# Fetching the second feed-forward block's weights at most 8 units ahead instead of 60

## The chip, the cores and the metric

The kernel runs on one core of one Trainium2 chip. Its time is the device time of one execution, in microseconds (us). Before the change three runs took 660.59, 662.50 and 663.89 us; the median is 662.5 us. Five parts of the core appear below: PE (TensorE, matrix multiplication), DVE (VectorE), ACT (ScalarE), POOL (GpSimd) and SP (SyncE, which here only issues DMA transfers).

## The reference

Attention with a position bias is followed by two feed-forward blocks over 1152 tokens of width 512, all in float32:

```python
attn = softmax(q k^T / 8 + bias(log-distance MLP)) @ v      # 2 batches, 8 heads, 576 positions, 64 wide
x    = attn, laid out as 1152 x 512
h    = x @ w_in                                              # 512 -> 2048
x    = (h * clip(h + 3, 0, 6) / 6) @ w_out                   # 2048 -> 512
xn   = x / sqrt(mean(x*x) + 1e-6) * rms_g
out  = (silu(xn @ w_gate) * (xn @ w_val)) @ w_out2           # 512 -> 1536 -> 512
```

The weights arrive as float64 arrays, and the kernel reads them as pairs of 32-bit integers.

## The kernel before

Tokens are cut into three blocks of 384 (n = 0, 1, 2), and the inner width of each feed-forward block into slices of 128 (16 slices in the first block, 12 in the second). A unit is one token block with one slice. There are 84 units: 0 to 47 belong to the first block, 48 to 83 to the second. Each block first goes through its slices with n = 0 and 1 (units 48 to 71 in the second block, two units to a slice) and then with n = 2 (units 72 to 83).

Every product is computed with operands split into a high and a low part (`wh`, `wl` for weights; `nh`, `nl` for the normalised tokens; `gh`, `gl` for the inner activations), as high x high, high x low and low x high. In the second block a unit therefore works as follows.

- Line 701 (`first`): 12 matmuls of 384 columns for the gate slice into a PSUM tile `h`, then 12 more for the value slice into another. Only two `h` tiles exist and they are used in turn.
- Line 729: ACT computes silu of the gate tile into `r`, which frees that `h` tile. Line 733: DVE multiplies `r` with the value tile, which frees the second one.
- Line 710: ACT makes `gh` out of `r`; line 713: DVE makes `gl`.
- Line 746 (`second`): 9 matmuls of 512 columns with the output weights. They are issued one unit late, so PE's order is gate and value of unit i, then the output matmuls of unit i-1, then gate and value of unit i+1.

Weights have to be converted from float64 to `wh` and `wl` before use. One weight tile of 128 x 512 is one transfer of 512 KB (line 110) into one of three `raw` buffers, and then goes through a small pipeline of turns, one stage a turn: ACT takes the absolute value of the upper words (line 130); DVE does three integer operations on it (lines 138, 139 and 143), the last of which frees the raw buffer; ACT rounds it to `wh` (line 122) and POOL subtracts to get `wl` (line 151). A turn carries at most one weight tile in each stage. A unit of the second block has two turns. In the first, lines 138, 139 and 143 stand on DVE ahead of line 733. In the second, lines 138 and 139 stand between lines 733 and 713, and line 143 behind line 713. If no weight is pending, the turn leaves these operations out.

Which weight is pending is decided while the program is built. 29 slots hold converted weights. After each unit, `weight_want` (lines 183 to 203) looks at the units from now on, up to `far` of them, for the first weight that is in no slot, picks the slot whose content is needed last, and issues the transfer. It goes on until three weights are pending. A slot whose content is needed again is taken only where the new weight is needed within 8 units (`near`).

In units 49 to 57 there is further work for the tokens of block n = 2, which reach the second block later than the others: three copies on DVE (line 768) beside ACT squares after unit 49, a square root on ACT, which needs a table load and another back to silu at line 729 (after unit 50), five tiny operations and three scalings on DVE (lines 784 to 796, after unit 51), and after each of the units 54 to 57 three transposes on PE (line 804, shown as `xnT`), then `nh` on ACT (line 805) and `nl` on DVE (line 810). These transposes take an `h` tile. So there the gate matmuls of the next unit wait for line 733 of this one, and its value matmuls wait for line 810.

All of this is written out in a fixed order for each engine.

Of the kernel before, what the change touches and what calls it, by code (L numbers as in the profile page):

```python
# [48 lines left out]
def kernel(ctx, tc, q, k, v, w1, b1, w2, w_in, w_out, w_gate, w_val, w_out2, rms_g, dtab, ntab, itab, out):  # L49
# [43 lines left out]
    pend = []  # L93
# [11 lines left out]
    def weight_load(wid, s):  # L105
        raw = wst.tile([128, 512, 2], I32, tag="raw", name="raw")
        dst = raw.rearrange("p c z -> p (c z)")
        if wid[0] in "igv":
            dst = dst.rearrange("p (k f) -> p k f", k=4)
        nc.sync.dma_start(out=dst, in_=weight_src(wid))  # L110
        pend.append((wid, s, raw, turn_no[0]))
# [68 lines left out]
    def next_use(w, u):  # L180
        return next((x for x in uses[w] if x >= u), INF)

    def weight_want(now, near, far):

        for u in range(now, min(now + far, len(seq))):
            for w in seq[u]:
                if w in where:
                    continue
                best, dist = None, -1
                for s, h in enumerate(holds):  # L190
                    d = INF + 1 if h is None else next_use(h, now)
                    if d > dist and (d >= INF or (d > u and u - now <= near)):
                        best, dist = s, d
                if best is None:
                    return False
                if holds[best] is not None:
                    del where[holds[best]]
                    slot_of.pop(holds[best], None)
                holds[best] = w
                where[w] = best  # L200
                weight_load(w, best)
                return True
        return False

    def weight_need(u):
        for w in seq[u]:
            assert w in where, (u, w)
            while not (w in slot_of and slot_of[w][2] == where[w]):
                late_turns.append((u, w))
                conv_turn()  # L210
# [11 lines left out]
    if True:  # L222
# [575 lines left out]
        def norm_5(n, c):  # L798
            if n < 2:
                ps = ps_y.tile([128, BT], F32, tag="yb", name="xnT")  # L800
            else:
                ps = ps_h.tile([128, BT], F32, tag="h", name="xnT")
            for t in range(3):
                transpose(ps[:, t * 128:(t + 1) * 128], xn_t[n, t][:, c * 128:(c + 1) * 128])
            nc.scalar.activation(out=x_t[1, n][0][:, c, :], in_=ps, func=ACTF.Copy, scale=rg[:, c:c + 1])
            return ps

        def norm_6(n, c, ps):
            h_, l_ = x_t[1, n]
            nc.vector.scalar_tensor_tensor(  # L810
                out=l_[:, c, :], in0=ps, scalar=rg[:, c:c + 1], in1=h_[:, c, :], op0=ALU.mult, op1=ALU.subtract,
            )
# [21 lines left out]
        def finish(ph, n, f, g):  # L834
            F = (F1, F2)[ph]
            last = (ph, n, f) == units[-1]
            second("ou"[ph], ph, n, f, F, g, last)
            if f == F - 1 and not last:
                if ph == 0:
                    late1.append(None)  # L840
                    late1.extend(part(norm_1, n, t) for t in range(3))
                    late1.append(None)
                    late.extend([None, None, part(norm_2, n)])
                    late.append(None)
                    late.append(part(norm_3, n))
                    late.extend(part(norm_4, n, t) for t in range(3))
                    late.append(None)
                    late.append(None)
                    late.append(lambda: turn.extend((n, c) for c in range(4)))
                else:  # L850
                    late1.append(None)
                    late1.extend(part(final, n, t) for t in range(3))

        def late_step():

            for q in (late1, late):
                while q and q[0] is not None:
                    q.pop(0)()
                if q:
                    q.pop(0)  # L860

        queue = []
        with tc.manual_schedule():
            for i, (ph, n, f) in enumerate(units):
                weight_need(i)
                g = (unit1, unit2)[ph](n, f)
                queue.append((ph, n, f, g))
                while len(queue) > (2 if ph == 0 else 1):
                    finish(*queue.pop(0))
                if turn:  # L870
                    x = turn.pop(0)
                    norm_6(*x, norm_5(*x))
                late_step()
                while len(pend) < 3 and weight_want(i + 1 - len(queue), 8, 60):
                    pass
            for x in queue:
                finish(*x)
            while late or late1:
                late_step()
# [31 lines left out]
```

## Time and profile before

| | |
|---|---|
| median of three runs | 662.5 us |
| the profiled execution's own time | 662.26 us |
| its span in the profile | 660.5 us |
| PE busy | 633.3 us (96%) |
| DVE busy | 479.8 us (73%) |
| ACT busy | 342.6 us (52%) |
| POOL busy | 144.7 us (22%) |
| unit 48, first matmul | 417.56 us |
| weight tiles converted | 86 |

The span is the time from the first to the last instruction that the profile holds; all times in the rows below count from its start. Matmuls overlap each other in the pipeline, so PE's busy time says less than the distance between the starts of its matmuls. The TensorE clock was granted in full in the whole span (0.999).

### The profile page before, as it was taken

To read this page: it belongs to the slowest core of one execution; us is meant where nothing else is said; L and a number is where in the kernel's file an instruction comes from. 1 tells how busy PE (TensorE), PEld (TensorE's weight loads), DVE (VectorE), ACT (ScalarE), POOL (GpSimd) and SP (SyncE) were. 2 spreads that over 40 slices of the span, in tenths; PEclk is the share of its full clock that TensorE was granted. 3 is DMA by queue.
4 is the path that set the end of the run, shared out by engine and by line. 5 is a ranking of instruction groups with operands and counts; after the bars stand their busy time and mean duration, and the time that the engine had idled before them with its cause. 6 is when DMAs were issued, how large, how long until landed. Compare 5 with 4: busy or idle time off the path is not lost.

```text
span 660.5 us, 11012 instructions
## 1 busy us (share of the span) xinstructions
PE 633.3 (96%) x4174; PEld 525.0 (79%) x4174; DVE 479.8 (73%) x885; ACT 342.6 (52%) x675; POOL 144.7 (22%) x117
## 2 busy tenths in 40 slices
PE   5699999999999999999999999999899999999997
PEld 2256656656777999999999989998789999999996
DVE  6687799758656799888843799989993552498512
ACT  5867766677556555555534555574542331354311
POOL 1000010013110243333310023333441130044300
PEclk9999999999999999999999999999999999999999
DMA  6999958537500144333320124444452230146101
GB/s 153 282 287 239 266 164 261 131 80 204 140 3 1 55 139 133 127 126 126 128 64 1 33 96 128 143 149 129 153 160 65 79 114 1 63 153 230 34 0 49
DMA packets 75250, 80.69 MB, mean 122 GB/s; under 512 B 23996, under 2 KB 59964, under 8 KB 75196
## 3 DMA queue, kind: packets, MB, share of 16 engines
q1 hardware_dynamic: 75196, 79.98, 40.8%
q8 instruction: 33, 0.54, 0.3%
q14 instruction: 21, 0.17, 0.1%
HBM read 66.71 MB, written 13.25 MB: 121 GB/s over the span
## 4 chain that ended last, share of the span: by engine, by line
PE 80%; DVE 11%; DMA 3%; issue 3%; ACT 1%; SPq 1%; DVEq 0%; ACTq 0%
PE h L701 33%; PE ya L746 16%; PE yb L746 8%; PE pv L490 6%; PE tps L86 6%; PE s L427 6%; PE bps L357 4%; DVE wm L139 2%; DVE e L441 1%; DVE wm L143 1%; DVE wm L138 1%; DMA bias<-biasd 1%; PE qps L86 1%; DMA raw<-in_moe_w_out_dram 1%; DVE R L344 1%
## 5 line engine op out<-in xcount | busy, mean ns | idle before, releaser
L151 POOL TENSOR_TENSOR wl<-wm,wh 128x512 fp32r<-128x512 f32 x86 | 126.4, 1470 | 301.1 <-ACT wh L122 176.2
L143 DVE SCALAR_TENSOR_TENSOR wm<-raw,wm 128x512 int32<-128x512 int32 x86 | 127.5, 1482 | 0.9
L710 ACT CAST gh<-r 128x384 fp32r<-128x384 f32 x84 | 43.2, 514 | 118.0 <-DVE r L733 71.2
L701 PE MATMUL h<-nh,wh 128*128 128x384 f32 x288 | 97.6, 339 | 5.1 <-DVE r L733 3.2
L701 PE MATMUL h<-nh,wl 128*128 128x384 f32 x288 | 96.7, 336 | 0.0
L701 PE MATMUL h<-nl,wh 128*128 128x384 f32 x288 | 96.5, 335 | 0.0
L441 DVE CUSTOM_DVE_ANT_1 e<-s,bias 128x576 f32<-128x576 f32 x72 | 54.3, 755 | 29.8 <-PE tps L86 17.7
L733 DVE TENSOR_TENSOR r<-r,h 128x384 f32<-128x384 f32 x36 | 19.9, 551 | 66.6 <-PE h L701 66.3
L452 ACT ACTIVATE e<-e,m 128x576 f32<-128x576 f32 x72 | 56.0, 778 | 19.8 <-DVE m L441 19.8
L701 PE MATMUL h<-xh,wh 128*128 128x384 f32 x192 | 65.4, 341 | 0.0
L701 PE MATMUL h<-xh,wl 128*128 128x384 f32 x192 | 64.7, 337 | 0.0
L139 DVE SCALAR_TENSOR_TENSOR wm<-raw,wm 128x512 int32<-128x512 int32 x86 | 62.5, 727 | 2.9
L701 PE MATMUL h<-xl,wh 128*128 128x384 f32 x192 | 64.4, 336 | 0.0
L701 PEld LDWEIGHTS h<-nh,wh 128*128 128x128 f32 x288 | 54.1, 188 | 8.6 <-DVE r L733 4.0
L130 ACT ACTIVATE wm<-raw 128x512 f32<-128x512 f32 x86 | 58.0, 674 | 5.1 <-DMA raw<-in_moe_w_in_dram 2.2
L713 DVE TENSOR_TENSOR gl<-r,gh 128x384 fp32r<-128x384 f32 x84 | 46.6, 554 | 15.6 <-ACT gh L710 15.6
L427 PE MATMUL s<-kS,q 64*128 64x288 f32 (+1 forms) x320 | 54.6, 449 | 2.7 <-DVE m L441 2.7
L86 PEld LDWEIGHTS tps<-ident,e 128*128 128x128 f32 x324 | 42.5, 200 | 18.2 <-issue 8.9
L86 PE MATMUL tps<-ident,e 128*128 128x128 f32 x324 | 55.9, 297 | 0.1
L344 DVE TENSOR_SCALAR R<-T,NB 128x368 f32<-128x368 f32 (+17 forms) x124 | 54.0, 485 | 2.2 <-PE bps L357 1.7
L122 ACT CAST wh<-wm 128x512 fp32r<-128x512 f32 x86 | 52.9, 617 | 4.7 <-DVE wm L143 4.7
L701 PEld LDWEIGHTS h<-nl,wh 128*128 128x128 f32 x288 | 54.1, 188 | 1.4
(102 smaller groups left out, 1079.6 us busy)
## 6 DMA issues: line engine op xcount, KB each, us to landing
raw<-in_moe_w_out_dram SPq DMA_DIRECT2D x33, 512.0 KB, 3.6
biasd<-ev SPq DMA_DIRECT2D x36, 295.5 KB, 4.1
raw<-in_moe_w_gate_dram SPq DMA_DIRECT2D x19, 512.0 KB, 3.5
raw<-in_moe_w_in_dram SPq DMA_DIRECT2D x18, 512.0 KB, 3.6
bias<-biasd SPq DMA_DIRECT2D x15, 576.0 KB, 5.4
raw<-in_moe_w_val_dram SPq DMA_DIRECT2D x16, 512.0 KB, 3.6
rawq<-in_q_dram SPq DMA_DIRECT2D x32, 128.0 KB, 3.3
bias<-biasd SPq DMA_DIRECT2D x10, 288.0 KB, 4.9
```

The source lines that it names most:

```text
L86: nc.tensor.transpose(out, in_, ident[:n, :n])
L122: nc.scalar.copy(out=hi, in_=m)
L130: nc.scalar.activation(out=m, in_=raw[:, :, 1].bitcast(F32), func=ACTF.Abs, scale=2.0 ** -112)
L139: nc.vector.scalar_tensor_tensor(out=m, in0=raw[:, :, 0], scalar=29, in1=m, op0=ALU.logical_shift_right, op1=ALU.bitwise_or,)
L143: nc.vector.scalar_tensor_tensor(out=m, in0=raw[:, :, 1], scalar=-0x80000000, in1=m, op0=ALU.bitwise_and, op1=ALU.bitwise_or,)
L151: nc.gpsimd.tensor_tensor(out=lo, in0=m, in1=hi, op=ALU.subtract)
L344: nc.vector.tensor_scalar(out=R, in0=src, scalar1=NB1[:, col], scalar2=None, op0=ALU.max)
L427: nc.tensor.matmul(s[sl, r, :SH], lhsT=q_t[t][h // 4][rows, h % 4, sl], rhs=kS[b][rows, h, :], start=True, stop=True,)
L441: nc.vector.tensor_tensor_reduce(out=e_t[u][:, a, :].rearrange("p (j r) -> p r j", r=2), in0=s[:, :, :SH], in1=bt[u][:, a, :].rearrange("p ...
L452: nc.scalar.activation(out=e_t[u][:, a, :], in_=e_t[u][:, a, :], func=ACTF.Exp, scale=-1.0, bias=m_t[t][:, h:h + 1], accum_out=sum_t[t][:, ...
L701: nc.tensor.matmul(ps, lhsT=w[wz][:, c * 128:(c + 1) * 128], rhs=x[xz][:, c, :], start=(i == 0), stop=(i == 11),)
L746: nc.tensor.matmul(y_t[ph, n, t], lhsT=g[gz][:, t * 128:(t + 1) * 128], rhs=w[wz], start=(f == 0 and i == 0), stop=(f == F - 1 and i == 2),)
```

## The change

The last argument of `weight_want`, the number of units to look ahead, becomes 8 in the second block. It stays 60 in the first.

```diff
                 late_step()
-                while len(pend) < 3 and weight_want(i + 1 - len(queue), 8, 60):
+                while len(pend) < 3 and weight_want(i + 1 - len(queue), 8, 60 if ph == 0 else 8):
                     pass
```

Up to unit 49 both programs stand in the same order. With 60, every unit from 48 to 57 carries two conversions on DVE, units 58 to 65 carry eight among them, and units 66 to 70 none. With 8, weights are asked for once every two units, three at a time: units 48 and 49 still carry two conversions each, unit 50 none, and units 51 to 66 three for every two units, two in each odd unit and one in each even unit (24 in these eight pairs, as many as units 50 to 65 carry before). One tile fewer is converted in all (85 in place of 86). The three places below show this on DVE. In the rows `wm` is the weight tile in conversion, `r`, `gl` and `nl` are as above, and `L733` marks each unit's multiplication.

On DVE behind unit 49, before: the three copies for block n = 2 and then units 50 and 51.

```order
L768 COPY xn<-ya 128x512 x3
L138 TENSOR_SCALAR wm<-wm 128x512
L139 SCALAR_TENSOR_TENSOR wm<-raw,wm 128x512
L143 SCALAR_TENSOR_TENSOR wm<-raw,wm 128x512
L733 TENSOR_TENSOR r<-r,h 128x384
L138 TENSOR_SCALAR wm<-wm 128x512
L139 SCALAR_TENSOR_TENSOR wm<-raw,wm 128x512
L713 TENSOR_TENSOR gl<-r,gh 128x384
L143 SCALAR_TENSOR_TENSOR wm<-raw,wm 128x512
L775 TENSOR_SCALAR a<-ss 128x3
```

And there now:

```order
L768 COPY xn<-ya 128x512 x3
L733 TENSOR_TENSOR r<-r,h 128x384
L713 TENSOR_TENSOR gl<-r,gh 128x384
L775 TENSOR_SCALAR a<-ss 128x3
L138 TENSOR_SCALAR wm<-wm 128x512
L139 SCALAR_TENSOR_TENSOR wm<-raw,wm 128x512
L143 SCALAR_TENSOR_TENSOR wm<-raw,wm 128x512
L733 TENSOR_TENSOR r<-r,h 128x384
```

Both conversions of unit 50 have gone from between the copies and line 775.

On DVE from unit 54's multiplication to unit 55's, before:

```order
L733 TENSOR_TENSOR r<-r,h 128x384
L138 TENSOR_SCALAR wm<-wm 128x512
L139 SCALAR_TENSOR_TENSOR wm<-raw,wm 128x512
L713 TENSOR_TENSOR gl<-r,gh 128x384
L143 SCALAR_TENSOR_TENSOR wm<-raw,wm 128x512
L810 SCALAR_TENSOR_TENSOR nl_4989<-xnT,rg,nh_4988 128x384
L138 TENSOR_SCALAR wm<-wm 128x512
L139 SCALAR_TENSOR_TENSOR wm<-raw,wm 128x512
L143 SCALAR_TENSOR_TENSOR wm<-raw,wm 128x512
L733 TENSOR_TENSOR r<-r,h 128x384
```

And there now:

```order
L733 TENSOR_TENSOR r<-r,h 128x384
L713 TENSOR_TENSOR gl<-r,gh 128x384
L810 SCALAR_TENSOR_TENSOR nl_4965<-xnT,rg,nh_4964 128x384
L138 TENSOR_SCALAR wm<-wm 128x512
L139 SCALAR_TENSOR_TENSOR wm<-raw,wm 128x512
L143 SCALAR_TENSOR_TENSOR wm<-raw,wm 128x512
L733 TENSOR_TENSOR r<-r,h 128x384
```

One of the two conversions is gone from this stretch; from unit 55's multiplication to unit 56's there are two, as before.

On DVE from unit 59's multiplication on, before, to that of unit 61:

```order
L733 TENSOR_TENSOR r<-r,h 128x384
L713 TENSOR_TENSOR gl<-r,gh 128x384
L138 TENSOR_SCALAR wm<-wm 128x512
L139 SCALAR_TENSOR_TENSOR wm<-raw,wm 128x512
L143 SCALAR_TENSOR_TENSOR wm<-raw,wm 128x512
L733 TENSOR_TENSOR r<-r,h 128x384
L713 TENSOR_TENSOR gl<-r,gh 128x384
L733 TENSOR_TENSOR r<-r,h 128x384
```

And now, to that of unit 60:

```order
L733 TENSOR_TENSOR r<-r,h 128x384
L138 TENSOR_SCALAR wm<-wm 128x512
L139 SCALAR_TENSOR_TENSOR wm<-raw,wm 128x512
L713 TENSOR_TENSOR gl<-r,gh 128x384
L143 SCALAR_TENSOR_TENSOR wm<-raw,wm 128x512
L138 TENSOR_SCALAR wm<-wm 128x512
L139 SCALAR_TENSOR_TENSOR wm<-raw,wm 128x512
L143 SCALAR_TENSOR_TENSOR wm<-raw,wm 128x512
L733 TENSOR_TENSOR r<-r,h 128x384
```

Here a second conversion has come in, and units 61 to 65 go on in the same manner.

## Rows read from the trace of the kernel before

**Rows 1.** Windows of two stretches: length, busy times, clock, DMA share, GB/s.

```profile
core 0: us, PE busy (x) PEld busy (x) DVE busy (x) ACT busy (x) POOL busy (x), PEclk, DMA share, GB/s
460.00:492.50 32.50, 29.02 (x152) 25.51 (x150) 32.05 (x43) 16.59 (x32) 13.15 (x10) 1.00 0.48 157
505.00:555.00 50.00, 50.00 (x266) 46.86 (x265) 21.91 (x34) 15.08 (x29) 9.77 (x7) 1.00 0.25 75
```

**Rows 2.** Chain of waits: start, length, what.

```profile
404.18 0.33 PE xnT L86 x3
...
496.99 4.18 PE h L701 x24
...
501.18 2.08 PE ya L746 x9
```

**Rows 3.** Timeline of PE: first gate matmul of units 50, 55, 60; delayed value matmuls.

```profile
start us, us, engine line op out<-in xcount [idle before <-releaser]
432.13 0.33 PE L701 MATMUL h<-nh,wh 128*128 128x384 f32 x1
...
454.76 0.45 PE L701 MATMUL h<-nh,wh 128*128 128x384 f32 x1 [1.56 <-DVE r L733]
...
467.66 0.44 PE L701 MATMUL h<-nh,wh 128*128 128x384 f32 x1 [1.68 <-DVE r L733]
...
471.41 0.44 PE L701 MATMUL h<-nh,wh 128*128 128x384 f32 x1 [1.38 <-DVE nl L810]
...
503.10 0.33 PE L701 MATMUL h<-nh,wh 128*128 128x384 f32 x1
```

**Rows 4.** Timeline of DVE, units 50 to 56 (L733 of units 50, 51, 52, 53, 55, 56).

```profile
434.03 1.87 DVE L768 COPY xn<-ya 128x512 f32<-128x512 f32 x3
...
438.46 0.55 DVE L733 TENSOR_TENSOR r<-r,h 128x384 f32<-128x384 f32 x1
...
444.40 0.55 DVE L733 TENSOR_TENSOR r<-r,h 128x384 f32<-128x384 f32 x1 [0.30 <-ACT r L729]
...
445.47 1.07 DVE L138 TENSOR_SCALAR wm<-wm 128x512 int32<-128x512 int32 x1 [0.52 <-ACT wm L130]
...
454.15 0.55 DVE L733 TENSOR_TENSOR r<-r,h 128x384 f32<-128x384 f32 x1
...
459.03 1.66 DVE L143 SCALAR_TENSOR_TENSOR wm<-raw,wm 128x512 int32<-128x512 int32 x1
460.62 0.54 DVE L733 TENSOR_TENSOR r<-r,h 128x384 f32<-128x384 f32 x1
...
474.04 0.55 DVE L733 TENSOR_TENSOR r<-r,h 128x384 f32<-128x384 f32 x1
...
477.75 0.60 DVE L810 SCALAR_TENSOR_TENSOR nl<-xnT,rg,nh 128x384 fp32r<-128x384 f32 x1
...
481.15 0.54 DVE L733 TENSOR_TENSOR r<-r,h 128x384 f32<-128x384 f32 x1
```

**Rows 5.** Timeline of DVE, units 61 and 62, then 76 and 77.

```profile
513.82 0.56 DVE L733 TENSOR_TENSOR r<-r,h 128x384 f32<-128x384 f32 x1 [4.57 <-PE h L701]
...
520.08 0.56 DVE L733 TENSOR_TENSOR r<-r,h 128x384 f32<-128x384 f32 x1 [2.67 <-PE h L701]
...
607.82 0.56 DVE L733 TENSOR_TENSOR r<-r,h 128x384 f32<-128x384 f32 x1 [0.48 <-PE h L701]
...
612.76 0.69 DVE L143 SCALAR_TENSOR_TENSOR wm<-raw,wm 128x512 int32<-128x512 int32 x1
614.08 0.56 DVE L733 TENSOR_TENSOR r<-r,h 128x384 f32<-128x384 f32 x1 [0.63 <-PE h L701]
```

**Rows 6.** Timeline of POOL: two subtractions, in units 53 and 76.

```profile
458.67 1.48 POOL L151 TENSOR_TENSOR wl<-wm,wh 128x512 fp32r<-128x512 f32 x1 [1.29 <-ACT wh L122]
...
606.74 1.74 POOL L151 TENSOR_TENSOR wl<-wm,wh 128x512 fp32r<-128x512 f32 x1 [1.75 <-ACT wh L122]
```

**Rows 7.** Timeline of ACT: the table load back to silu, and nh of unit 55.

```profile
442.58 1.28 ACT L729 ACT_TABLE_LOAD   x1
...
476.21 0.59 ACT L805 ACTIVATE nh<-xnT,rg 128x384 fp32r<-128x384 f32 x1
```

**Rows 8.** The raw tiles from 417 us on: time from issue to landing.

```profile
DMA to landing us min/median/max: 3.3/3.6/5.1
```

## The prediction

> **What bounds the kernel now.** I first read the windows, to see which engine waits where. From 505 to 555 us, in the second block, PE is busy all 50 us and DVE 21.91 of 50; from 460 to 492.5 PE is busy only 29.02 of 32.5 and DVE 32.05 [rows 1]. So inside one block, doing the same matmuls, PE sets the pace in one stretch and DVE in the other. The clock is 1.00 in both, so it is not a slower PE.
>
> The chain of waits then gives PE's own pace: 4.18 us for the 24 gate and value matmuls and 2.08 for the 9 output matmuls, 6.27 us a unit, and 0.33 for a set of three transposes [rows 2]. PE's timeline shows what the DVE stretch costs. Unit 50 starts its first gate matmul at 432.13, unit 60 at 503.10: 70.97 us for ten units. At PE's pace they would take 62.70, and the four sets of transposes behind units 54 to 57 add 1.32, together 64.02. **6.95 us are lost there.** The largest single waits stand in the rows: unit 53's value matmuls at 454.76 and unit 55's gate matmuls at 467.66, both released by line 733, and unit 55's value matmuls at 471.41, released by line 810 [rows 3]. Behind unit 60 nothing more is lost: line 733 stands at 513.82 for unit 61 and 614.08 for unit 77, 100.26 us for sixteen units, again 6.27 each [rows 5]. More than these 6.95 us can't come back in the block.
>
> Last I read DVE's timeline for what fills it [rows 4, 5]. When PE does not wait, line 733 starts 4.45 us behind its unit's first gate matmul (513.82 less 503.10 less 6.27) [rows 3, 5]. Unit 50's could start at 436.58 and starts at 438.46; unit 52's could start at 449.1 and starts at 454.15 [rows 4]. DVE is behind, and this is what PE ends up waiting for.
>
> **What the change does, part by part.** *The conversion.* From unit 61's line 733 to unit 62's there is one conversion and DVE idles 2.67 us; in the interval before there is none and it idles 4.57 [rows 5]. So a conversion alone costs DVE 1.90 us. When POOL's subtraction runs beside one of the three operations, that one gets longer: line 143 takes 0.69 us alone [rows 5] and 1.66 where the subtraction of 458.67 overlaps it [rows 4, 6], 0.97 more.
>
> *Two kinds of interval.* In the steady pattern of the change, from an odd unit's line 733 to the even one's there are two conversions and two subtractions, as from unit 52 to 53 now: 6.47 us (454.15 to 460.62) [rows 4]. From an even unit's to the odd one's there is one conversion and at most one subtraction in its way: 6.26 less 2.67 idle, plus 0.97, is 4.56 [rows 5]. A pair costs DVE 11.03 us of PE's 12.53. With line 810 (0.60) in each it is 7.11 (474.04 to 481.15, measured) and 5.16, 12.27 of PE's 13.19 [rows 2, 4]. Before, two long intervals followed each other: 12.94 and 14.2. So DVE falls from above PE's pace to below it, in all eight pairs (units 51 to 66).
>
> *The start.* Unit 50 loses both its conversions. The copies end at 435.90, so its line 733 starts when PE allows, at 436.58, instead of 1.88 late [rows 4]. Unit 51's could start at 442.85. What delayed it before was the table load that ended at 443.86, which stands behind line 775 and so moves earlier with it, by about the same 1.9 us and the conversion behind line 733 [rows 4, 7]; I take 442.85. From unit 51's to unit 52's line 733 DVE does the same work as before, two conversions, the tiny operations and the scalings: 9.75 us (444.40 to 454.15), of which 0.52 waited for ACT, late from the table loads [rows 4]. That puts line 733 of unit 52 at 442.85 + 9.23 = 452.08, its end at 452.63. PE needs it for unit 53's value matmuls at 444.67 + 6.27 + 2.09 = 453.03: no wait, with 0.4 us to spare. Then 4.56 to unit 53 (456.64; 1.3 late) and 6.47 to unit 54 (463.11, end 463.66), needed by unit 55's gate matmuls at 457.21 + 6.27 + 0.33 = 463.81. No wait, but 0.15 to spare.
>
> *The transposes.* In unit 54 line 810 can't start before `nh`, which ends 2.76 us behind line 733 now (474.04 to 476.80) [rows 4, 7], so it ends near 463.11 + 2.76 + 0.60 = 466.5. Unit 55's value matmuls want it at 465.9: 0.6 lost. In the odd units 55 and 57 the conversion still stands ahead of line 810, which ends 4.31 behind line 733 (474.04 to 478.35) [rows 4] and so 8.76 behind the unit's first gate matmul, where the next unit's value matmuls want it at 6.27 + 0.33 + 2.09 = 8.69. A tenth is lost twice, and about as much again in restarting PE, which I put at 0.1 from the longer first matmuls of the delayed groups (0.44 and 0.45 for 0.33) [rows 3]. Together 0.6 + 0.1 + 2 x 0.2 = 1.1 at the slow end and, if unit 52 comes half a microsecond sooner, 0.4. I take the middle, 0.7.
>
> *Line 810 beside a subtraction.* In the even units 54 and 56 POOL's subtraction of the second turn now may run while line 810 wants to start; no row shows these two together. From above it costs 0.97 in each, of which some 0.3 is spare: 1.3 in all. From below nothing: line 733 of unit 76, at 607.82 for 0.56 us, ran wholly inside the subtraction of 606.74 to 608.48 and was no longer than others [rows 5, 6]; it reads one operand from PSUM and one from SBUF, as line 810 does. That is the nearer row; I take 0. The Trainium skill's page "SBUF — State Buffer", section "Who interferes with whom", says that a VectorE instruction with two SBUF inputs contends with GpSimd, and one with at most one SBUF input outside the two-port modes does not. By that rule line 810 would cost nothing; if it did contend the time would be 1.3 us above my forecast. The trace agrees for line 733 (0.56 us beside a subtraction).
>
> *Transfers.* They get later relative to their use, but landing takes 5.1 us at most [rows 8], and in the written order no weight is finished later than four units (25 us) ahead of its use. Cost 0; the cover is those four units. Moving ACT's and POOL's share of the conversions costs nothing either: together they stay far below PE (16.59 and 13.15 of 32.5 us where two conversions a unit run) [rows 1]. The one conversion fewer (86 to 85) falls among the last units, where PE does not wait: 0.
>
> **Sum.** 6.95 given back, 0.7 kept: 6.25 us. Against the profiled execution's own 662.26 (its span 660.5 and 1.8 around it, which does not change) that makes 656.0. The median of the runs, 662.5, is 0.2 above the profiled one, below what can be told apart. The forecast's own bounds are 655.3 (all 6.95) and 657.3 (1.3 more kept).
>
> **Rivals.**
> - *The transposes stay bound by DVE.* If the four intervals of units 54 to 57 remain as long as now (7.11 against PE's 6.60, 0.5 each, 2.0 in all, on top of half a microsecond from unit 52), 2.5 of 6.95 stay: 657.8. For it: line 810 waits behind a conversion in every second unit, and the slack worked out above is 0.15 to 0.4 us. Against it: the long intervals alternate with ones of 5.16.
> - *The lag comes from the norm work, not the conversions.* The longest interval, 9.75, holds the same work after the change. If unit 52's line 733 is as late as now, the waits at 454.76, 467.66 and 471.41 stay, some 1.7 + 1.8 + 1.5 = 5.0 by their idle and restart [rows 3]; then 1.9 are gained: 660.3. Against it: unit 51 starts 1.55 sooner.
> - *The conversions moved into units 59 to 66 become the bound: slower.* PE waits for nothing there now. With one subtraction shutting out one DVE operation a pair costs 11.03. If each shut out two (0.97 more for each of three), it would cost 13.94 against 12.53, 1.41 lost in each of eight pairs, 11.3 in all: 662.26 - 6.25 + 11.3 = 667.3. It decides from 13.3 a pair on (12.53 + 6.25/8). Against it: the measured interval with two subtractions is 6.47, one lengthened operation each.
>
> That the change does not do what it says is out: the order of DVE shows the conversions moved.
>
> **How the numbers follow.** The forecast, 656.0, gets 0.66; the transposes 0.16 (657.8); the norm work 0.13 (660.3); slower 0.05 (667.3). The range for 8 in 10 takes the first two cases and the spread of the runs before (1.9 below and 1.4 above their median): 654.0 to 659.2. What a measurement of this kernel can tell from no change is about 0.5%, 3.3 us: faster than 659.2 are the first two cases, 0.82; within 0.5%, 0.13; slower, 0.05.
>
> **What would show it.** Right: unit 60's first gate matmul at about 496.9 in place of 503.10; PE busy all of the stretch behind 442 us but for waits on line 810 of a few tenths; line 733 of units 53 and later no more than 2 us behind its unit's matmuls; DVE idle in every pair from 58 on. Wrong: a wait of over 1 us at unit 53's or 55's matmuls (the norm work), waits on line 810 in all of units 55 to 58 (the transposes), any PE wait on line 733 behind unit 59 (slower), or ACT waiting on a raw tile.

## The result, and the profile after

Over eight runs each, the changed kernel took 655.79 us and the kernel before 661.46; the ratio is 0.9908, with a 95% interval of 0.9890 to 0.9927. That is 5.7 us between the two medians, 6.1 by the ratio. The prediction was 656.0.

The profile read here is of an execution of 656.09 us; its unit 50 starts within 0.02 us of that of before. Another execution, of 659.37 us, came to unit 48 3.4 us later (420.96 for 417.58) and spends the same 64.7 us on the ten units 50 to 59 (435.53 to 500.27).

The windows of the same two stretches, in the same columns as [rows 1]:

```profile
460.00:492.50 32.50, 32.50 (x174) 29.49 (x173) 24.02 (x38) 15.07 (x29) 11.88 (x8) 1.00 0.42 130
505.00:555.00 50.00, 50.00 (x265) 46.87 (x264) 28.05 (x42) 17.22 (x33) 12.88 (x9) 1.00 0.31 96
```

PE, 29.02 of 32.5 before, is now busy throughout. DVE falls from 32.05 to 24.02 in the first stretch and rises from 21.91 to 28.05 in the second: conversions have moved from one to the other, where they meet no wait.

PE's timeline, unit 50, the value matmuls of units 55, 56 and 58, and unit 60, to compare with [rows 3]:

```profile
432.15 0.33 PE L701 MATMUL h<-nh,wh 128*128 128x384 f32 x1
...
466.08 0.44 PE L701 MATMUL h<-nh,wh 128*128 128x384 f32 x1
...
472.93 0.45 PE L701 MATMUL h<-nh,wh 128*128 128x384 f32 x1
...
486.38 0.45 PE L701 MATMUL h<-nh,wh 128*128 128x384 f32 x1
...
496.94 0.33 PE L701 MATMUL h<-nh,wh 128*128 128x384 f32 x1
```

The ten units 50 to 59 take 496.94 - 432.15 = 64.79 us, 0.77 over PE's pace of 64.02, where 6.95 over it stood before: 6.18 given back. From unit 60 to the end of the span nothing changed (157.4 us before and after). So the whole gain lies in these ten units. The three value groups in the middle are all that still waits, each 0.1 to 0.2 us (0.16, 0.13, 0.13) and 0.1 for the longer first matmul after it (0.44 and 0.45 for 0.33).

DVE's timeline, line 733 of units 50 to 56, one line 138 and line 810 of unit 54, to compare with [rows 4]:

```profile
436.61 0.55 DVE L733 TENSOR_TENSOR r<-r,h 128x384 f32<-128x384 f32 x1 [0.68 <-PE h L701]
...
442.87 0.55 DVE L733 TENSOR_TENSOR r<-r,h 128x384 f32<-128x384 f32 x1 [2.68 <-PE h L701]
...
451.61 0.55 DVE L733 TENSOR_TENSOR r<-r,h 128x384 f32<-128x384 f32 x1
...
453.83 1.06 DVE L138 TENSOR_SCALAR wm<-wm 128x512 int32<-128x512 int32 x1 [0.53 <-ACT wm L130]
...
456.26 0.55 DVE L733 TENSOR_TENSOR r<-r,h 128x384 f32<-128x384 f32 x1
...
462.71 0.54 DVE L733 TENSOR_TENSOR r<-r,h 128x384 f32<-128x384 f32 x1
...
465.41 0.62 DVE L810 SCALAR_TENSOR_TENSOR nl<-xnT,rg,nh 128x384 fp32r<-128x384 f32 x1 [1.02 <-ACT nh L805]
...
468.56 0.55 DVE L733 TENSOR_TENSOR r<-r,h 128x384 f32<-128x384 f32 x1 [0.75 <-PE h L701]
...
475.41 0.56 DVE L733 TENSOR_TENSOR r<-r,h 128x384 f32<-128x384 f32 x1 [0.75 <-PE h L701]
```

The brackets are what to read: DVE now waits for PE in units 50, 51, 55 and 56, where it waited for nothing from PE before. The lag (how far line 733 stands behind the place that PE allows, 4.45 us after its unit's first gate matmul) is still 2.5 us in unit 52 (451.61), 0.9 in unit 53, 1.05 in unit 54, and gone in unit 55.

POOL's timeline, the subtraction in unit 54:

```profile
464.40 1.29 POOL L151 TENSOR_TENSOR wl<-wm,wh 128x512 fp32r<-128x512 f32 x1 [2.16 <-DVE gl L713]
```

It ends at 465.69, with line 810 running since 465.41 and lasting 0.62, hardly longer than elsewhere (0.60). The two overlap for 0.28 us only.

The timeline of DVE and POOL, the second conversion of a long interval, first where DVE is late (unit 53 to 54) and then where it is not (unit 59 to 60):

```profile
460.77 1.47 POOL L151 TENSOR_TENSOR wl<-wm,wh 128x512 fp32r<-128x512 f32 x1 [1.29 <-ACT wh L122]
461.13 1.67 DVE L143 SCALAR_TENSOR_TENSOR wm<-raw,wm 128x512 int32<-128x512 int32 x1
...
500.01 0.69 DVE L143 SCALAR_TENSOR_TENSOR wm<-raw,wm 128x512 int32<-128x512 int32 x1
500.32 1.54 POOL L151 TENSOR_TENSOR wl<-wm,wh 128x512 fp32r<-128x512 f32 x1 [1.95 <-ACT wh L122]
...
501.39 0.55 DVE L733 TENSOR_TENSOR r<-r,h 128x384 f32<-128x384 f32 x1 [0.69 <-PE h L701]
```

In the first case POOL starts 0.36 us ahead of line 143, which takes 1.67. In the second it starts 0.31 behind, line 143 takes 0.69, and DVE then idles 0.69. In this program POOL's subtraction follows ACT's rounding, which stands behind ACT's silu, and silu follows PE (silu starts at 459.52 and 499.24, both times released by PE, and the subtraction 1.25 and 1.08 us later). So a DVE that is late comes upon a subtraction that is already running. Two conversions cost 6.45 us in the first interval and 5.57 (6.26 less 0.69) in the second.

### The profile page after: what moved, and what is told of

Same layout as the page of the kernel before. It is cut to its first block, busy times and chain, and to the rows that moved or that the text cites. A ratio compares the mean times of both kernels' runs of the same rounds, so it can differ in the third digit from the quotient of the medians.

```text
span 657.6 us, 11000 instructions
## 1 busy us (share of the span) xinstructions
PE 636.8 (97%) x4174; PEld 527.3 (80%) x4174; DVE 473.4 (72%) x882; ACT 341.8 (52%) x673; POOL 143.9 (22%) x116
## 4 chain that ended last, share of the span: by engine, by line
PE 90%; DVE 4%; DMA 3%; SPq 1%; issue 1%; ACT 0%; DVEq 0%
PE h L701 38%; PE ya L746 18%; PE yb L746 9%; PE pv L490 6%; PE s L427 6%; PE tps L86 6%; PE bps L357 4%; DVE e L441 1%; DMA bias<-biasd 1%; PE qps L86 1%; DMA raw<-in_moe_w_out_dram 1%; PE kps L86 1%; PE rps L86 1%; DVE R L344 1%; DVE et L472 1%
## 5 line engine op out<-in xcount | busy, mean ns | idle before, releaser
L143 DVE SCALAR_TENSOR_TENSOR wm<-raw,wm 128x512 int32<-128x512 int32 x85 | 121.6, 1430 | 0.9
L733 DVE TENSOR_TENSOR r<-r,h 128x384 f32<-128x384 f32 x36 | 19.9, 553 | 63.2 <-PE h L701 63.2
L701 PE MATMUL h<-xh,wl 128*128 128x384 f32 x192 | 64.7, 337 | 0.0
L139 DVE SCALAR_TENSOR_TENSOR wm<-raw,wm 128x512 int32<-128x512 int32 x85 | 59.8, 704 | 2.8
L427 PE MATMUL s<-kS,q 64*128 64x288 f32 (+1 forms) x320 | 56.6, 464 | 1.2 <-DVE m L441 1.2
L701 PEld LDWEIGHTS h<-nh,wl 128*128 128x128 f32 x288 | 54.0, 188 | 0.0
```

What stands on the lines that cost most here:

```text
L139: nc.vector.scalar_tensor_tensor(out=m, in0=raw[:, :, 0], scalar=29, in1=m, op0=ALU.logical_shift_right, op1=ALU.bitwise_or,)
L143: nc.vector.scalar_tensor_tensor(out=m, in0=raw[:, :, 1], scalar=-0x80000000, in1=m, op0=ALU.bitwise_and, op1=ALU.bitwise_or,)
L427: nc.tensor.matmul(s[sl, r, :SH], lhsT=q_t[t][h // 4][rows, h % 4, sl], rhs=kS[b][rows, h, :], start=True, stop=True,)
L701: nc.tensor.matmul(ps, lhsT=w[wz][:, c * 128:(c + 1) * 128], rhs=x[xz][:, c, :], start=(i == 0), stop=(i == 11),)
```

## Experiments

The theory behind them: at two conversions a unit DVE needs 6.47 us for PE's 6.27, because POOL's subtraction shuts it out once per conversion; together with the norm work it falls behind, and PE ends up waiting. The measure in all of them is the time from unit 50's to unit 60's first gate matmul, "the ten units" in all that follows, read from each run's own profile (70.97 before, 64.79 after, 64.02 at PE's pace).

**Only the start.**

```diff
-                while len(pend) < 3 and weight_want(i + 1 - len(queue), 8, 60):
+                while len(pend) < 3 and weight_want(i + 1 - len(queue), 8, 8 if 48 <= i < 54 else 60):
```

> Looks 8 units ahead behind units 48 to 53 and 60 elsewhere, so that units 50 to 55 carry conversions as after the change and units 56 to 59 two each (56 to 59, then the rest as before). Measure: from unit 50's to unit 60's first gate matmul, 70.97 us before, 64.74 after, 64.02 at PE's own pace. Theory (DVE falls behind at the start, where two conversions a unit meet the norm work, and at 6.47 us a unit never catches up): the start is mended, so 65.2 to 66.0, from waits on line 810 in units 57 and 58 only; whole time within 0.3% of the change. Rival A (the norm work alone makes the lag): 70 to 71. Rival B (the transposes with two conversions a unit make most of the loss): 67 to 68.

Measured: 64.99 us for the ten units (431.29 to 496.28), and a ratio to before of 0.9908 (0.9888 to 0.9927), that of the change itself. The expected 65.2 was missed by 0.2 us. PE's timeline, the first gate matmuls of units 50 and 60, and DVE's, line 733 of units 57 and 58:

```profile
431.29 0.33 PE L701 MATMUL h<-nh,wh 128*128 128x384 f32 x1
...
496.28 0.33 PE L701 MATMUL h<-nh,wh 128*128 128x384 f32 x1
```

```profile
481.36 0.56 DVE L733 TENSOR_TENSOR r<-r,h 128x384 f32<-128x384 f32 x1 [0.73 <-PE h L701]
...
488.20 0.56 DVE L733 TENSOR_TENSOR r<-r,h 128x384 f32<-128x384 f32 x1 [0.73 <-PE h L701]
```

Between these two lines stand two conversions and line 810, and DVE still waits 0.73 us for PE: they cost 6.11 us here, not the 7.11 that units 55 to 56 take before. Thinning out units 50 to 55 alone gives back all that can be told apart. So 6.47 us for two conversions, which the theory takes for granted, is the price where DVE is late; where it enters without a lag, two a unit do no harm.

**Only the rest.**

```diff
-                while len(pend) < 3 and weight_want(i + 1 - len(queue), 8, 60):
+                while len(pend) < 3 and weight_want(i + 1 - len(queue), 8, 8 if i >= 54 else 60):
```

> Looks 60 units ahead up to unit 53 and 8 from unit 54 on: two conversions a unit up to unit 55 as before, none in units 56 to 58, then three for two units. Theory: the waits at unit 53's and 55's matmuls (1.7, 1.8 and 1.5 us) stay and only the small waits on line 810 behind unit 55 go: 69.0 to 69.6 us for the ten units, about 1.5 us faster than before in all. Rival A (norm work alone): 70 to 71. Rival B (the transposes): 65 to 67.

PE's timeline, the three waits that [rows 3] shows in the kernel before:

```profile
455.87 0.44 PE L701 MATMUL h<-nh,wh 128*128 128x384 f32 x1 [1.55 <-DVE r L733]
...
468.77 0.44 PE L701 MATMUL h<-nh,wh 128*128 128x384 f32 x1 [1.68 <-DVE r L733]
...
472.52 0.44 PE L701 MATMUL h<-nh,wh 128*128 128x384 f32 x1 [1.40 <-DVE nl L810]
```

They are all there to within 0.02 us. The ten units take 69.99 (433.25 to 503.24), 0.4 above the expected range: I had left out the restart of 0.1 behind each wait and the short wait of unit 56. It touches the lower edge of rival A, so this run does not separate A; the next one does. Rival B (65 to 67) falls. The whole time did not measurably move (ratio 1.0001, 0.9987 to 1.0016, so at most 0.9 us faster): the 1.5 us expected of it did not come, and the 0.98 of the ten units does not show in it.

**Without the norm work.**

```diff
 def norm_2(n):
+    if n == 2:
+        return
     ...
```

The same test in the functions behind it leaves only two tiles made for n = 2 and none of its scalings.

> The kernel before without the square root, the tiny operations and the scalings for token block n = 2 (lines 775 to 796; its tokens stay unscaled); copies, transposes and line 810 stay, and so do two conversions a unit. Theory: line 733 of unit 50 is still 1.9 late from the copies and two conversions, each unit adds 0.2 and each transposed one 0.5, so some 4 us stay lost: about 68.0 us for the ten units (67 to 69). Rival A (the norm work alone): 64.0 to 64.8. Rival B (transposes): 66 to 67.

DVE's timeline, line 733 of units 50 to 54:

```profile
437.48 0.55 DVE L733 TENSOR_TENSOR r<-r,h 128x384 f32<-128x384 f32 x1
...
443.95 0.54 DVE L733 TENSOR_TENSOR r<-r,h 128x384 f32<-128x384 f32 x1
...
450.42 0.54 DVE L733 TENSOR_TENSOR r<-r,h 128x384 f32<-128x384 f32 x1
...
456.88 0.54 DVE L733 TENSOR_TENSOR r<-r,h 128x384 f32<-128x384 f32 x1
...
463.34 0.54 DVE L733 TENSOR_TENSOR r<-r,h 128x384 f32<-128x384 f32 x1
```

No brackets: DVE never waits, and its intervals are 6.46 to 6.47 us, the price of two conversions with nothing else. Against PE's 6.27 it loses 0.2 a unit. The ten units take 68.18 (431.15 to 499.33), as expected, and 4.16 of 6.95 us stay lost. So the norm work is worth 2.8 us of the loss and cannot be the whole of it: rival A falls. What remains begins in unit 50, whose line 733 is 1.88 us late (437.48 for 435.60) behind the three copies and its two conversions; no run takes the copies away.

**Without POOL beside DVE.**

```diff
-nc.gpsimd.tensor_tensor(out=lo, in0=m, in1=hi, op=ALU.subtract)
+if turn_no[0] >= 79:
+    nc.scalar.copy(out=lo, in_=m)
+else:
+    nc.gpsimd.tensor_tensor(out=lo, in0=m, in1=hi, op=ALU.subtract)
```

> The kernel before, but from unit 48 on POOL's subtraction (line 151) is replaced by a copy on ACT (the low part then holds a rounded copy of the weight instead of the remainder), so that POOL does nothing beside DVE; look-ahead and the number of conversions stay. Theory: each conversion costs DVE 1.90 instead of 2.87 us, two conversions a unit come to 4.9 of PE's 6.27, and DVE is no longer behind: 64.0 to 64.8 us for the ten units, the time of the changed kernel. Rival C (what counts is the number of conversions in a unit or how far ahead they are fetched, not the time that POOL takes from DVE): 69 to 71.

DVE's timeline, unit 53's line 733, the last conversion step ahead of unit 54's line 733 (here line 736):

```profile
454.84 0.56 DVE L736 TENSOR_TENSOR r<-r,h 128x384 f32<-128x384 f32 x1 [0.41 <-ACT wl L152]
...
458.63 0.69 DVE L143 SCALAR_TENSOR_TENSOR wm<-raw,wm 128x512 int32<-128x512 int32 x1
461.11 0.56 DVE L736 TENSOR_TENSOR r<-r,h 128x384 f32<-128x384 f32 x1 [1.79 <-ACT wl L152]
```

Two conversions still stand in this interval, at the old look-ahead, and DVE idles 1.79 us of it; line 143 takes 0.69. (The bracket names ACT, but line 736 starts 4.45 us behind its unit's first gate matmul of 456.66, where PE allows.) Unit 52's line is still 1.4 us late (449.96), and unit 53's is not late any more: without the subtractions DVE catches up within one unit. The ten units take 63.97 us (431.59 to 495.56), PE's pace; the ratio is 0.9894 (0.9871 to 0.9916). Two conversions a unit fit, and the fetch distance and the number of conversions are not what costs in themselves; rival C falls. What costs is the time that they take of DVE, subtractions included, where DVE is already late.

**The subtraction on DVE itself.**

```diff
-nc.gpsimd.tensor_tensor(out=lo, in0=m, in1=hi, op=ALU.subtract)
+(nc.vector if turn_no[0] >= 79 else nc.gpsimd).tensor_tensor(out=lo, in0=m, in1=hi, op=ALU.subtract)
```

> The kernel before (60 units ahead, two conversions a unit), but from unit 48 on the subtraction of line 151 is done by DVE instead of POOL: DVE gets one operation more per conversion (about 0.65 us) and nothing runs beside it. Theory (what POOL takes from DVE, 0.97 us a conversion, is part of what put DVE above PE's pace): a two-conversion interval comes to 5.7 us, 6.2 with line 810, below PE's 6.27 and 6.60, and one wait of about 0.9 on line 810 is left from the start: 64.5 to 66 us from unit 50's to unit 60's first gate matmul (70.97 before, 64.74 after), the time of the change within 0.3%. Rival D (DVE is bound by its own operations, and more of them make it worse): over 72 us.

Measured: 65.02 us for the ten units (431.62 to 496.64), ratio 0.9915 (0.9900 to 0.9929). DVE does one operation more per conversion and is faster for it: its intervals with two conversions are 5.60 and 5.59 us (units 52 to 54), where they were 6.47 and 6.44; rival D falls. PE's timeline, unit 55's value matmuls, shows a wait where one was expected:

```profile
466.33 0.44 PE L701 MATMUL h<-nh,wh 128*128 128x384 f32 x1 [0.58 <-ACT r L729]
```

Its size (0.75, and 0.86 with the longer restart, for 0.9) fits; unit 55's gate matmuls are 0.2 late too. Its cause is not shown. The expected one is line 810, but that ends at 466.61 by the record, after the group has started at 466.33; the record names ACT's silu, which ends at 466.28.

**Twice the subtraction, after the change.**

```diff
     nc.gpsimd.tensor_tensor(out=lo, in0=m, in1=hi, op=ALU.subtract)
+    if turn_no[0] >= 83:
+        nc.gpsimd.tensor_tensor(out=lo, in0=m, in1=hi, op=ALU.subtract)
```

> As the change, but from unit 50 on POOL does each subtraction twice (the same result). This is the slower rival of the prediction, made on purpose: if every subtraction shuts out one operation of DVE, a pair of units costs DVE 13.9 us instead of 11.0, over PE's 12.53, and 1.4 us are lost in each pair up to unit 66: 70 to 72 us for the ten units and 8 to 11 us in all. If the second subtraction of a pair falls where DVE waits anyway or DVE gets in between the two, the pair stays near 11 to 12.5: 64.7 to 66 us, 0 to 2 us in all.

DVE's timeline, line 733 (here 735) of units 58, 59 and 60, with the three conversion steps ahead of unit 60:

```profile
494.32 0.54 DVE L735 TENSOR_TENSOR r<-r,h 128x384 f32<-128x384 f32 x1
...
499.94 0.55 DVE L735 TENSOR_TENSOR r<-r,h 128x384 f32<-128x384 f32 x1
...
503.63 1.52 DVE L138 TENSOR_SCALAR wm<-wm 128x512 int32<-128x512 int32 x1
505.18 1.75 DVE L139 SCALAR_TENSOR_TENSOR wm<-raw,wm 128x512 int32<-128x512 int32 x1
506.96 1.66 DVE L143 SCALAR_TENSOR_TENSOR wm<-raw,wm 128x512 int32<-128x512 int32 x1
508.55 0.54 DVE L735 TENSOR_TENSOR r<-r,h 128x384 f32<-128x384 f32 x1
```

All three steps are lengthened, and the pair takes 14.23 us (494.32 to 508.55) for the 13.9 worked out: six subtractions in it, and six longer operations. The ten units take 70.35 (431.35 to 501.70), in the expected range. The whole time is 671.81, a ratio of 1.0165 (1.0148 to 1.0181): 11 us over before and 16 over the change, more than the expected 8 to 11 over the change. I had counted pairs up to unit 66 only. From unit 50 to unit 68 the profile loses 9.6 us against that of the change (124.51 for 114.92); the conversions of units 71 to 79 were doubled as well and cost three further waits of 1.17, 1.18 and 1.94 us. A pair of that price does bound the kernel, as the slower rival says; that one subtraction shuts out two operations, which it needs, is not so.

The same run has line 810 (here 812) wholly beside a subtraction. The timeline of DVE and POOL, unit 55:

```profile
476.53 1.61 POOL L153 TENSOR_TENSOR wl<-wm,wh 128x512 fp32r<-128x512 f32 x1
476.92 0.60 DVE L812 SCALAR_TENSOR_TENSOR nl<-xnT,rg,nh 128x384 fp32r<-128x384 f32 x1
```

**Six units ahead.**

```diff
-                while len(pend) < 3 and weight_want(i + 1 - len(queue), 8, 60):
+                while len(pend) < 3 and weight_want(i + 1 - len(queue), 8, 60 if ph == 0 else 6):
```

> As the change, but 6 units ahead: 79 weight tiles in place of 85, no conversions in units 50 to 52, then three for two units. Theory: PE is at its own pace already, so nothing is left to gain but the waits on line 810, which stay where an odd unit's conversion stands ahead of it: 64.3 to 64.8 us for the ten units, whole time within 0.3% of the change. Rival E (fewer transfers and conversions are worth time in themselves): 1% faster than the change.

Measured: 64.44 us for the ten units (430.61 to 495.05), 654.85 us and a ratio of 0.9902 (0.9887 to 0.9917) to before. Against 0.9908 of the change this is the same; six tiles fewer are worth nothing that can be told, as expected where PE does not wait. It beats the change by no measurable amount, and rival E falls.

**The change again.**

> The changed kernel once more, for its profile: 64.6 to 64.9 us for the ten units; unit 48's first gate matmul within 2 us of 417.6 (420.96 in the first profile of the changed kernel, whose instructions up to there are those of the kernel before), and a whole time of 654.5 to 656.5 us.

Measured: 64.79 us for the ten units, unit 48 at 417.58, and 656.09 us in all, each as expected.

## Why the prediction was right

- *The bound.* 6.95 us lost in ten units and none behind them: 6.18 came back there and nothing elsewhere.
- *The signs.* Unit 60's first gate matmul came at 496.94 for 496.9, no value group waited more than 0.16 us, line 733 is 0.9 and 1.05 us late in units 53 and 54 and on time from unit 55 on, and DVE idles in every pair from 58 on.
- *The intervals.* DVE fell below PE's pace as forecast, but not at the prices of the sum. Only the long interval where DVE is late (53 to 54) measured what was put on it, 6.45 for 6.47. Where DVE is not late, two conversions cost 5.57 us, not 6.47 (59 to 60), and 6.10 with line 810, not 7.11 (55 to 56: 6.85 less 0.75 idle), since the second subtraction meets no operation that it lengthens. The prediction took the price of a late DVE for all eight pairs. [rows 5] could have told: from unit 76 to 77 the kernel before has two conversions in 6.26 us and idles 0.63. The time did not depend on it, as PE sets the pace at either price.
- *Luck in the short ones.* Unit 52 to 53 measured 4.65 for 4.56, but of the 0.97 that were put on POOL 0.64 are a longer operation (line 138, 1.06 for 0.42); DVE also waited 0.53 for ACT. Unit 54 to 55 measured 5.10 without its 0.75 of idle, for 5.16, and no operation is longer there: DVE waited 1.02 for `nh`, where the sum had 0.97 for POOL.
- *The start.* Unit 50's line 733 is where PE allows, as worked out; unit 51's 442.87 for 442.85; unit 52's 451.61 for 452.08; unit 54's 462.71 for 463.11. Units 52 and 54 came sooner than the sum, which took the work between units 51 and 52 at its old length: before, two of its operations were lengthened (1.07 and 1.71), now one is (1.78).
- *The transposes.* 0.7 kept, 0.77 measured, but not made up as worked out. The slow end had 0.6 in unit 55 and a tenth each in 56 and 58 beside restarts; measured are 0.16, 0.13 and 0.13 us of wait and 0.11 of restart each. The 0.6 of the slow end shrank as unit 52 came 0.47 sooner; that the middle of my two ends met the total is partly luck.
- *Line 810 beside a subtraction.* I took 0 between 0 and 1.3. In the changed kernel itself the two hardly meet (0.28 us in unit 54, 0.03 in unit 56), as line 810 waits for `nh`; so the kernel's time does not test it. The run with doubled subtractions does: 0.60 us wholly beside POOL's work, as elsewhere. The Trainium skill's page "SBUF — State Buffer", section "Who interferes with whom", has a VectorE instruction with at most one SBUF input, outside the two-port modes, free of contention with GpSimd, and one with two SBUF inputs contending with a GpSimd instruction that reads SBUF. The trace agrees with both: line 810 keeps its 0.60, and line 143, with two, goes from 0.69 to 1.66 in the kernel before.
- *The rivals.* The norm work is part of the loss (2.8 us) but not its cause alone; the transposes add to a lag and do not make one (6.11 us for PE's 6.60 in the run with only the start). The slower case needs two shut-out operations for each subtraction; there is at most one.
- *What was off in size.* The 5.0 us that I put on the three waits in the rival of the norm work is 6.0 with the restarts and the small waits around them (69.99 less 64.02 in the run with the rest alone); and the price of a doubled subtraction was summed over too few units.

## What to carry to other kernels

Where a planner fills every turn as soon as something is free, look-ahead decides how dense the side work is. Compare the time per unit of the engine that carries it, the operations lengthened by POOL included, with the pace of the engine that should set the time, and read that price both where the engine is late and where it is not. Here the same two conversions cost 5.57 us a unit where DVE waited for PE and 6.47 where it was late, on either side of PE's 6.27. So a lag that one burst of work left did not wear off but grew by 0.2 us a unit (shown in the run without the norm work), and it was enough to thin out the side work where the burst stands.

## What was not expected of the hardware

In the run with doubled subtractions PE waited 3.08 us ahead of unit 55's gate matmuls. The windows around it show the granted clock (columns as in [rows 1]):

```profile
464.00:466.90 2.90, 0.01 (x1) 0.00 (x0) 2.87 (x3) 0.00 (x0) 1.95 (x2) 1.00 0.26 91
467.00:470.70 3.70, 3.61 (x12) 3.61 (x13) 2.10 (x4) 2.09 (x4) 2.44 (x2) 0.54 0.45 142
470.70:474.50 3.80, 3.80 (x21) 3.54 (x20) 3.04 (x6) 1.75 (x4) 0.12 (x1) 1.00 0.20 40
```

And PE's timeline there:

```profile
467.09 0.56 PE L703 MATMUL h<-nh,wh 128*128 128x384 f32 x1 [3.08 <-DVE r L735]
467.45 0.52 PE L703 MATMUL h<-nl,wh 128*128 128x384 f32 x1
467.77 0.52 PE L703 MATMUL h<-nh,wl 128*128 128x384 f32 x1
...
470.84 0.34 PE L703 MATMUL h<-nh,wh 128*128 128x384 f32 x1
471.02 0.34 PE L703 MATMUL h<-nl,wh 128*128 128x384 f32 x1
```

After this wait the clock is at 0.54, nearly all at its lower level of 1.2 GHz, and the matmuls start 0.32 us apart instead of 0.17 until 470.65. That is some 1.6 us of PE's time. After a wait of 1.94 us in the same run, and after all waits of up to 1.68 in units 50 to 59 of the kernel before, only the second matmul came late (0.28 behind the first), and the rest 0.17 apart.

The kernel loses less than the 1.6, though. Line 810 of unit 54, for which the value matmuls have to wait anyway, ends at 469.81, and the next line 733 (here 735) waits for PE only 0.66 us:

```profile
473.22 0.56 DVE L735 TENSOR_TENSOR r<-r,h 128x384 f32<-128x384 f32 x1 [0.66 <-PE h L703]
```

From there to PE's next long wait on line 735, at 523.30, DVE never waits for PE, so 0.66 us is an estimate of what the lower clock cost at most.
